# Forgetting attention and a GELU layer on one core: a new order of loads, casts, masks and fillers in the opening stage

## The chip, the cores and the metric

The kernel runs on one core of a Trainium2 chip. The core has five engines with a queue each: TensorE (PE in the profile; PEld are its weight loads), VectorE (DVE), ScalarE (ACT), GpSimd (POOL) and SyncE (SP). Each works through its own queue in order; semaphores between them make an instruction wait for another engine's result or for a DMA. The metric is the device time of one execution in microseconds; less is better.

## What is computed

For 8 batches of 8 heads, 576 tokens and head dimension 64, attention with a forget gate is computed; its output, as 4608 tokens of 512 features, goes through a two-layer network with a hidden width of 2048. Both matter here, since the network's first tokens are computed while the attention of later heads still runs.

```python
scores = scale * np.matmul(q, k.transpose(0, 1, 3, 2))
log_f = np.log(np.clip(f, 0.0001, 1.0))
cum = np.cumsum(log_f, axis=-1)
decay = cum[:, :, :, None] - cum[:, :, None, :]
scores = np.where(causal, -1000000000.0, scores + decay)
attn = softmax(scores)                       # over the keys
x = np.matmul(attn, v)                       # then (batch * seq, heads * dim)
...
h = x @ w_in
g = 0.5 * h * (1.0 + np.tanh(c * (h + 0.044715 * h * h * h)))
return (g @ w_out).astype(np.float32)
```

## The kernel before, in words

**Attention by quads.** A quad is four heads of one batch; quads 0 and 1 are batch 0, quads 2 and 3 batch 1, and so on to quad 15. The decay splits into a factor of the query, which cancels in the softmax, and a weight of the key, `exp(-cum)`. The kernel keeps these weights as `wT` (float32) and, rounded, as `w_bf` (bf16), and multiplies the values by them (`vw`). So a quad's result is a product of the exponentials (`pt`) with `vw`, divided by a product of `pt` with `w_bf`. For a quad TensorE computes scores into PSUM (`ps_s`, line 261), ScalarE turns them into `pt` (line 269), the blocks on the diagonal are masked either by GpSimd (`affine_select`, line 275) or by VectorE as a product with a triangle (line 304), and TensorE multiplies again (line 315 for quads 0 and 1, which are cut into a half 0 of 256 tokens and a half 1 of 320; line 329 for the others). VectorE makes the reciprocals of the denominators with two transpositions (`den`, line 348, and `rb`, line 352) and writes the result, times `rb`, to `xT` (line 360). Queries and keys come as `q_c` and `k_c` and are transposed by VectorE (line 197).

**The network by chunks** of 512 tokens. The first layer of chunk 0 is computed by halves and by four groups of hidden features (line 491, and line 514 for the piece that is copied to `snap` first), with GELU on ScalarE; its second layer is `mlp_out` (line 626): 4 row tiles of 16 products each, copied by VectorE and stored through SyncE. Later chunks use other functions that the change does not touch.

**An order written out by hand.** The scheduler is off. `setup()` issues the first loads and preparations, then `run(FRONT)` (line 781) goes through a table of words and issues each word's instructions to their engines' queues, so that the order of words is the order in each queue; words of different engines do not hold each other except by data. A word with `@` makes its first instruction wait also for the instruction kept under the name that follows. The words that the change and the prediction name:

- `B.n.c`: n filler products without use, c columns wide (line 239), on TensorE. Set-up issues 13 of its own.
- `Z`: zeros (line 675), copied by ScalarE from a zero tile into parts of `w_bf`, `vw` and `v_nat`. `CU`, `CW`, `SB`: the running sums of log f on TensorE and GpSimd and the exponentials that give `wT`. `W`: the cast of `wT` to `w_bf` on VectorE (line 724), of all quads, or with `.0` of quads 0 and 1, with `.1` of the others.
- `TQ.i`, `TK.i`: transposition of quad i's queries or keys. `LQ.i`, `LK.i`: their loads, issued by GpSimd.
- `LP.t`: load of tile t (128 tokens) of batch 0's values, issued by GpSimd; `LX`, `LV`: values of later batches, by GpSimd or SyncE. `WI.c`: one of 8 slices of `w_in` (two make a group of hidden features), `WO.c`: one of 4 quarters of `w_out`, both by GpSimd. Every load that GpSimd issues goes into one queue.
- `S.i.r`, `H.i.r.g`, `Q.i.r.g`: scores of quad i in round r with their exponentials, whole or by two heads.
- `M.i.r`: masks on GpSimd; `m.i.r`: masks on VectorE.
- `D.i`: denominators of quad i (product on TensorE, reciprocals on VectorE); `D.i.h` of half h. `V.i.x`, `v.i.x`, `V.i.x.h`: one of the two halves of the head dimension of the result, product on TensorE and the product with `rb` on VectorE.
- `vw.i`, `VW.i`: weighting of quad i's values on VectorE or GpSimd (line 214); with `.0` tiles 0 and 1, with `.1` tiles 2 to 4. `CL.i`: a copy within `vw` on VectorE.
- `h`, `j`, `J`, `E`: parts of chunk 0's first layer, its held pieces and their GELU. `F.c.n`, `f.c.n`: n products' worth of chunk c's second layer; `I`, `U`, `G`, `K`: of chunk 1.

PSUM tiles come from small pools: `psS` has two tiles of scores, `psO` one, `psM` two (`po_m`, `ps_q`, `pso`). A product into a new tile waits until the tile's former content has been read.

Of the kernel before, what the change touches and what calls it, by code (L numbers as in the profile page):

```python
# [16 lines left out]
def kernel(  # L17
# [192 lines left out]
    def make_vw(i, eng, part=None):  # L210
        h0 = 4 * (i % QPB)
        vb = v_nat[(i // QPB) % 2]
        t0, t1 = {None: (0, NT), 0: (0, QA // 128), 1: (QA // 128, NT)}[part]
        eng.tensor_mul(  # L214
            vw[i % 2][:, t0:t1], vb[:, t0:t1, h0:h0 + 4, :],
            wT[:, i, t0:t1, :].unsqueeze(3).to_broadcast([128, t1 - t0, 4, D]))
# [78 lines left out]
    def mask_by_product(i, r, keys=None):  # L295
        p = pt[i % 2]
        if i < 2:
            todo = [(0, col, n) for (key, col, n) in diagonals(r, keys)]
# [4 lines left out]
        for (m, col, n) in todo:
            nc.vector.tensor_mul(p[:, :, col:col + n], p[:, :, col:col + n],
                                 causal[m][:, 0:n].unsqueeze(1).to_broadcast([128, 4, n]))
# [339 lines left out]
    def setup():  # L645
# [16 lines left out]
        nc.vector.tensor_scalar(f_sb, f_sb, 1e-4, 1.0, op0=ALU.max, op1=ALU.min)
# [195 lines left out]
```

## Time and profile before

| what | value |
|---|---|
| median of 3 runs (lowest to highest) | 321.47 us (321.04 to 322.42) |
| the profiled execution | 321.33 us |
| its span, first to last instruction | 319.6 us |
| granted TensorE clock, mean | 0.999 |
| instructions | 12355 |

The profile is that of one execution. Its times are counted from the first instruction, and the span leaves out some 1.7 us around it. A line of a timeline has the start, the time it took, the engine, the source line, the operation, what it writes and reads, the shape, and how many equal instructions were merged; in brackets stands the idle time before it and what ended it. Products on TensorE overlap: a row of many has the time from the first start to the last end, and the next row can start a little before that end.

### The profile page before, as it was taken

The page shows a single profiled execution, that of the slowest core. Times are in us where ns is not written, and L with a number is a line of the kernel's source. Part 1 is how long each engine was busy: PE and PEld are TensorE (multiplying, and loading weights), DVE is VectorE, ACT ScalarE, POOL GpSimd, SP SyncE. Part 2 cuts the span into 40 slices and gives each one's busy share as a digit, 9 for nine tenths or more (in the row PEclk, how much of TensorE's full clock was granted, in tenths as well). Part 3 has the DMA queues.
Part 4 walks back from the last instruction along what each step waited for, and adds up shares of the span by engine and source line. Part 5 has one row for each costly group of instructions (what it writes and reads, how often), then busy time and mean ns, then how long its engine had stood idle before and what let it go on. Part 6 is the DMA issues. An engine that isn't in the chain of part 4 may idle for free.

```text
span 319.6 us, 12355 instructions
## 1 busy us (share of the span) xinstructions
PE 311.4 (97%) x5527; PEld 218.9 (68%) x5547; DVE 250.6 (78%) x398; ACT 208.4 (65%) x265; POOL 113.1 (35%) x160
## 2 busy tenths in 40 slices
PE   7899999999999999999999999999999999999995
PEld 3467744545776477766867677768766798788784
DVE  4866049977789899779987898689868969886882
ACT  6895676676766786759756865778567844722730
POOL 8997465720500219501770068104710240000000
PEclk9999999999999999999999999999999999999999
DMA  7999999898104830791159512971120112003013
GB/s 124 233 168 203 206 238 253 157 177 185 40 14 126 143 66 17 149 213 41 37 100 209 93 37 72 198 132 37 37 68 0 37 37 68 3 34 100 0 35 98
DMA packets 47574, 33.45 MB, mean 105 GB/s; under 512 B 29857, under 2 KB 42273, under 8 KB 47521
## 3 DMA queue, kind: packets, MB, share of 16 engines
q0 software_dynamic: 9712, 15.99, 28.9%
q1 hardware_dynamic: 37664, 16.60, 20.1%
q8 instruction: 43, 0.70, 0.9%
q10 hardware_dynamic: 144, 0.07, 0.1%
q14 instruction: 11, 0.08, 0.1%
HBM read 36.85 MB, written 9.44 MB: 145 GB/s over the span
## 4 chain that ended last, share of the span: by engine, by line
PE 93%; DVE 2%; DMA 2%; issue 1%; ACT 0%; POOL 0%; DVEq 0%; POOLq 0%
PE ps_w L565 30%; PE ps_h L374 16%; PE po L329 9%; PE ps_s L261 9%; PE ps_cd L433 8%; PE ps_ab L433 6%; PE ps_h L491 4%; PE pso L635 3%; PE ps_h L388 2%; DMA q_c<-in_q_dram 2%; PE po_m L315 2%; DVE qT L197 1%; PE ps_q L514 1%; PE idle_ps L239 1%; ACT pt L269 0%
## 5 line engine op out<-in xcount | busy, mean ns | idle before, releaser
L269 ACT ACTIVATE pt<-ps_s 128x1024 bf16<-128x1024 f32 (+2 forms) x98 | 92.3, 992 | 35.5 <-PE ps_s L261 31.9
L275 POOL TENSOR_SCALAR_AFFINE_SELECT pt<-pt 128x512 bf16<-128x512 bf16 (+2 forms) x67 | 40.3, 611 | 103.6 <-ACT pt L269 102.5
L374 PE MATMUL ps_h<-xT,w_in_sb 128*128 128x512 bf16 x228 | 54.5, 379 | 0.6
L565 PEld LDWEIGHTS <-gT 128*32 128x32 bf16 (+1 forms) x1247 | 50.6, 97 | 5.9 <-issue 1.7
L565 PE MATMUL ps_w<-w_out_sb,gT 128*32 128x256 bf16 (+1 forms) x1050 | 46.9, 273 | 0.0
L381 ACT ACTIVATE gT<-ps_h 128x1024 bf16<-128x1024 f32 x30 | 30.6, 1019 | 17.2 <-PE ps_h L374 16.7
L565 PEld LDWEIGHTS <-gsum 128*32 128x32 bf16 (+1 forms) x1256 | 39.3, 97 | 1.4
L374 PEld LDWEIGHTS <-w_in_sb 128*128 128x128 bf16 x240 | 23.4, 98 | 24.3 <-issue 0.4
L261 PE MATMUL ps_s<-qT,kT 32*128 32x448 bf16 (+5 forms) x880 | 35.4, 262 | 1.7 <-DVE qT L197 1.2
L214 POOL TENSOR_TENSOR vw<-v_nat,wT 128x1280 bf16<-128x1280 f32 (+1 forms) x13 | 29.8, 2291 | 3.8 <-DMA v_nat<-in_v_dram 3.4
L565 PE MATMUL ps_w<-usum,gsum 128*32 128x256 bf16 (+1 forms) x832 | 30.6, 273 | 0.0
L197 DVE STREAM_TRANSPOSE kT<-k_c 128x576 f32<-128x576 f32 x16 | 19.9, 1246 | 12.6 <-DMA k_c<-in_k_dram 12.6
L261 PEld LDWEIGHTS <-kT 32*128 32x128 bf16 x896 | 16.3, 92 | 18.5 <-issue 13.3
L442 ACT ACTIVATE gT<-snap 128x512 bf16<-128x512 f32 x45 | 26.1, 625 | 3.0 <-DVE snap L456 2.4
L590 DVE TENSOR_TENSOR o_st<-ps_w,snap 128x512 f32<-128x512 f32 x31 | 21.3, 686 | 8.3 <-PE ps_w L565 7.2
L433 PEld LDWEIGHTS <-w_in_sb 128*128 128x128 bf16 x240 | 23.4, 98 | 6.2 <-issue 1.5
L329 PE MATMUL po<-pt,vw 128*32 128x64 bf16 (+4 forms) x624 | 22.5, 278 | 0.3 <-DVE den L348 0.3
L360 DVE TENSOR_TENSOR xT<-po,rb 128x576 bf16<-128x576 f32 x26 | 19.5, 751 | 2.9 <-PE po L329 2.3
L329 PEld LDWEIGHTS <-vw 128*32 128x32 bf16 x672 | 14.5, 97 | 10.5 <-issue 4.4
L433 PEld LDWEIGHTS <-xT 128*128 128x128 bf16 x180 | 17.6, 98 | 5.2
L197 DVE STREAM_TRANSPOSE qT<-q_c 128x576 f32<-128x576 f32 x16 | 19.9, 1244 | 0.5 <-DMA q_c<-in_q_dram 0.5
L191 POOL DMA_DIRECT2D k_c<-in_k_dram x16 | 9.2, 577 | 25.0 <-DVE qT L197 21.0
(111 smaller groups left out, 482.8 us busy)
## 6 DMA issues: line engine op xcount, KB each, us to landing
out_dram<-o_st SPq DMA_DIRECT2D x35, 256.0 KB, 2.3
k_c<-in_k_dram POOLq DMA_DIRECT2D x16, 288.0 KB, 6.0
q_c<-in_q_dram POOLq DMA_DIRECT2D x16, 288.0 KB, 6.4
v_nat<-in_v_dram SPq DMA_DIRECT2D x16, 256.0 KB, 6.5
v_nat<-in_v_dram SPq DMA_DIRECT2D x20, 128.0 KB, 5.2
w_in_sb<-in_moe_w_in_dram POOLq DMA_DIRECT2D x8, 256.0 KB, 7.2
w_out_sb<-in_moe_w_out_dram POOLq DMA_DIRECT2D x4, 512.0 KB, 9.7
v_nat<-in_v_dram POOLq DMA_DIRECT2D x9, 128.0 KB, 5.9
```

What stands on the lines that cost most here:

```text
L197: nc.vector.transpose(out=dst.rearrange("p s c -> p (s c)").bitcast(FP32) .rearrange("p (t a) -> p a t", a=S // 32), in_=src.rearrange("p ...
L214: eng.tensor_mul(vw[i % 2][:, t0:t1], vb[:, t0:t1, h0:h0 + 4, :], wT[:, i, t0:t1, :].unsqueeze(3).to_broadcast([128, t1 - t0, 4, D]))
L261: nc.tensor.matmul(tiles[h // 2][:, h % 2, c0:c0 + nq], key_columns(i, key, h, c), qq[32 * h:32 * h + 32, q0:q0 + nq, c], start=(c == 0 an ...
L269: nc.scalar.activation(p[:, 2 * g:2 * g + 2, off:off + n], t[:, :, 0:n], AF.Exp, scale=scale)
L275: nc.gpsimd.affine_select(out=x, in_=x, compare_op=ALU.is_ge, fill=0.0, base=0, pattern=pattern, channel_multiplier=-1)
L329: nc.tensor.matmul(po[r0:r0 + w.shape[-1], 448 + q0:448 + q0 + nq], w, p[:, h, col:col + nq], start=(key in (0, "low")), stop=(key in ("lo ...
L374: nc.tensor.matmul(ph[:, j, :], w_in_sb[:, dt, 128 * ft:128 * ft + 128], xT[:, dt, CH * c:CH * (c + 1)], start=(dt == 0), stop=(dt == N_DT ...
L381: nc.scalar.activation(gT[:, 2 * pr:2 * pr + 2, :], ph, AF.Gelu_apprx_tanh)
L433: nc.tensor.matmul(ps[:, j], w[:, dt, 128 * j:128 * j + 128], x[:, dt], start=(first and j == 0 and dt == 0), stop=(dt == 1), skip_group_c ...
L442: nc.scalar.activation(gT[:, ft:ft + 2, HC * j:HC * (j + 1)], x, AF.Gelu_apprx_tanh)
L565: nc.tensor.matmul(ps[c0:c0 + width, n, cols[0]:cols[1]], x[:, j, 128 * n + c0:128 * n + c0 + width], w[:, j, cols[0]:cols[1]], start=(fir ...
L590: nc.vector.tensor_add(st, ps, kept[name])
```

## The change

Five things are done.

1. The zeros are written by five memsets of VectorE within `setup()`, ahead of the clamp of f, in place of ScalarE's five copies; the word `Z` is gone.
2. On GpSimd's queue `LP.4` is issued ahead of the masks `M.0.0`, `WI.3` ahead of the masks of quad 1, and `LP.3` behind these and in front of `WI.4`.
3. On VectorE, `W` casts quads 0 and 1 alone at first; the others' cast comes behind half 1 of batch 0. `vw.0.1` goes behind the two copies of `ps_q`. Quad 2's denominators go ahead of `TK.4` and `TQ.4`. Fillers are moved: one less ahead of `S.0.0`, two more behind `CW`, one less behind `D.1.0`.
4. `mlp_out` starts two row tiles at once: 12 products of each, then the last 4 of each; the other two as before. The words `F.0.n` between the scores of quad 2 are cut anew (6, 10, 9, 10 become 7, 9, 10, 9).
5. Quad 3's masks of round 0 are on GpSimd (`M.3.0`, two masks) in place of VectorE (`m.3.0`). `m.3.1` on VectorE comes sooner in the table, and `VW.3`, the weighting on GpSimd, waits for it by a semaphore; `CL.3` follows later.

```diff
     SETUP = """
-        Z.1.2 TK.0 LP.0 LP.1
+        TK.0 LP.0 LP.1
     """
     FRONT = """
-        TQ.0 B.3.384 TR TK.1 SB Z.0.3.4 CU B.3.384 S.0.0 CW H.0.2.0 H.0.2.1 B.6.384 TQ.1 W WI.0 WI.1 vw.0.0 LP.2@LQ.0 M.0.0 LP.4 LP.3 WI.2 H.1.0.1
-        H.1.0.0 vw.1.0 M.1.0.1 M.1.0.0 WI.3 WI.4 WI.5 D.0.0 B.2.384 H.1.1.1 V.0.0.0 H.0.1.1 V.0.1.0 H.0.1.0 D.1.0 B.1.384 V.1.0.0 M.0.1 WI.6 WI.7
-        H.1.1.0 M.1.1 V.1.1.0 Q.0.3.0 vw.0.1 h.0.0.0 h.0.0.0 M.0.3 LQ.2 LK.2 Q.1.3.1 h.0.0.1 h.0.0.1 S.1.2 M.1.3 VW.1.1 WO.0 D.0.1 j.0.1 j.0.1 j.0.1
-        j.0.1 E.0.0 j.0.1 V.0.1.1 V.0.0.1 D.1.1 J.0.2 WO.1 V.1.1.1 V.1.0.1 J.0.3 J.1.0 WO.2@WI.7 WO.3 J.1.1 TQ.2 LK.3 LQ.3 J.1.2 J.1.3 LX.1.0@WO.0
-        LQ.4 TK.2 X F.0.6 LK.4 TK.3 S.2.0 M.2.0 LK.5 F.0.10 S.2.2 M.2.2 LX.1.1@WO.2 F.0.9 S.2.1 TQ.3 F.0.10 LV.2.0@LK.5 m.2.1 vw.2 TQ.4 TK.4 S.3.0
-        f.0.1 CL.2 LQ.5 VW.3 D.2 f.0.6 S.3.1 F.0.6 V.2.0 m.3.0 S.3.2 TK.5 LK.6 M.3.2 f.0.7 V.2.1 CL.3 S.4.1 m.3.1 LQ.6 F.0.6 TQ.5 H.4.2.1 D.3
+        TQ.0 B.3.384 TR TK.1 SB CU B.2.384 S.0.0 CW B.2.384 H.0.2.0 H.0.2.1 B.6.384 TQ.1 W.0 WI.0 WI.1 vw.0.0 LP.2@LQ.0 LP.4 M.0.0 WI.2 WI.3 H.1.0.1
+        H.1.0.0 vw.1.0 D.0.0 M.1.0.1 M.1.0.0 LP.3 WI.4 WI.5 B.2.384 H.1.1.1 V.0.0.0 H.0.1.1 V.0.1.0 H.0.1.0 D.1.0 V.1.0.0 M.0.1 WI.6 WI.7 H.1.1.0
+        V.1.1.0 M.1.1 Q.0.3.0 h.0.0.0 h.0.0.0 M.0.3 LQ.2 LK.2 Q.1.3.1 h.0.0.1 h.0.0.1 vw.0.1 S.1.2 M.1.3 VW.1.1 WO.0 D.0.1 j.0.1 j.0.1 j.0.1 j.0.1
+        E.0.0 j.0.1 V.0.1.1 V.0.0.1 D.1.1 J.0.2 WO.1 V.1.1.1 V.1.0.1 J.0.3 W.1 J.1.0 WO.2@WI.7 WO.3 J.1.1 TQ.2 LK.3 LQ.3 J.1.2 J.1.3 LX.1.0@WO.0
+        LQ.4 TK.2 X F.0.7 LK.4 TK.3 S.2.0 M.2.0 LK.5 F.0.9 S.2.2 M.2.2 LX.1.1@WO.2 F.0.10 S.2.1 TQ.3 F.0.9 LV.2.0@LK.5 m.2.1 vw.2 S.3.0 f.0.1 CL.2
+        LQ.5 M.3.0 D.2 TK.4 f.0.6 S.3.1 F.0.6 m.3.1 VW.3@m.3.1 V.2.0 TQ.4 S.3.2 TK.5 LK.6 M.3.2 f.0.7 V.2.1 S.4.1 LQ.6 F.0.6 TQ.5 CL.3 H.4.2.1 D.3
...
     def mlp_out(c):
-        for n in range(CH // 128):
+        tiles, late = {}, 3 * N_FT // 4
+        for (n, f0, f1) in ((0, 0, late), (1, 0, late), (0, late, N_FT), (1, late, N_FT), (2, 0, N_FT), (3, 0, N_FT)):
             r0 = CH * c + 128 * n
-            st = ostage_pool.tile([128, D_MODEL], FP32, name="o_st", tag="o")
-            pso = psM.tile([128, D_MODEL], FP32, name="pso", tag="m")
-            for ft in range(N_FT):
+            if f0 == 0:
+                tiles[n] = psM.tile([128, D_MODEL], FP32, name="pso", tag="m")
+            pso = tiles[n]
+            for ft in range(f0, f1):
...
                 if ft == N_FT - 1:
+                    st = ostage_pool.tile([128, D_MODEL], FP32, name="o_st", tag="o")
                     nc.vector.tensor_copy(st, pso)
...
-    def zeros(which):
-        todo = [(w_bf[0:64, :, LOW, :], idle[0:64, 0:BH].rearrange("p (i h) -> p i h", h=4))]
...
-        for n in which:
-            nc.scalar.copy(*todo[n])
+    def zeros():
+        nc.vector.memset(w_bf[0:64, :, LOW, :], 0.0)
+        for t_ in vw:
+            nc.vector.memset(t_[0:64, LOW, :, :], 0.0)
+        for t_ in v_nat:
+            nc.vector.memset(t_[64:128, HIGH, :, :], 0.0)
```

`make_vw` and `mask_by_product` now return their instructions, so that `VW.3@m.3.1` has something to tie together.

More of the change, by code (lines that the diff above doesn't have):

```diff
@@ L302, in mask_by_product @@
                     and rounds[r][0] <= col < rounds[r][0] + 512 and key != 0]
[L303 to L305 removed]
+        return [nc.vector.tensor_mul(p[:, :, col:col + n], p[:, :, col:col + n],
+                                     causal[m][:, 0:n].unsqueeze(1).to_broadcast([128, 4, n])) for (m, col, n) in todo]
     def product(i, groups, spare, part=None):
@@ L661, in setup @@
             nc.vector.memset(t_[:, 64 + S:], 0.0)
+        zeros()
         nc.vector.tensor_scalar(f_sb, f_sb, 1e-4, 1.0, op0=ALU.max, op1=ALU.min)
```

5 lines of the change are left out of this document (1 added, 4 removed).

## The prediction

> **What bounds the kernel now.** I read the engines' busy times and the chain first, then TensorE's instructions in order of time, then those of the engines that end its waits.
>
> ```profile
> PE 311.4 (97%) x5527; PEld 218.9 (68%) x5547; DVE 250.6 (78%) x398; ACT 208.4 (65%) x265; POOL 113.1 (35%) x160
> ...
> PE 93%; DVE 2%; DMA 2%; issue 1%; ACT 0%; POOL 0%; DVEq 0%; POOLq 0%
> ```
>
> TensorE is busy for 97% of the span and holds 93% of the chain that ended last. The change takes no product away, so it can only close gaps in TensorE's queue or open some. Every edit lies ahead of the first product of chunk 1 (about 64 us), so I look for gaps there.
>
> ```profile
> 1.26 3.92 PE L239 MATMUL idle_ps<-usum 128*128 128x384 bf16 x13 [1.26 <-DVE usum L654]
> ...
> 8.71 0.52 PE L261 MATMUL ps_s<-qT,kT 32*128 32x256 bf16 x16 [1.22 <-DVE qT L197]
> 9.17 0.70 PE L703 MATMUL cum_ps<-gsum 128*128 128x256 f32 x2
> 10.13 0.46 PE L261 MATMUL ps_s<-qT,kT 32*128 32x320 bf16 x4 [0.27 <-ACT pt L269]
> ...
> 11.22 1.15 PE L239 MATMUL idle_ps<-usum 128*128 128x384 bf16 x6
> ...
> 16.44 0.34 PE L239 MATMUL idle_ps<-usum 128*128 128x384 bf16 x1
> ...
> 18.30 1.04 PE L514 MATMUL ps_q<-xT,w_in_sb 128*128 128x256 bf16 x8
> ...
> 19.88 1.05 PE L514 MATMUL ps_q<-xT,w_in_sb 128*128 128x256 bf16 x8
> ...
> 21.30 0.96 PE L315 MATMUL po_m<-pt,w_bf 128*32 128x320 bf16 x20
> ...
> 25.36 0.70 PE L315 MATMUL po_m<-pt,w_bf 128*32 128x320 bf16 x20
> ...
> 48.69 0.85 PE L329 MATMUL po<-pt,w_bf 128*32 128x512 bf16 x24
> ...
> 53.08 0.87 PE L329 MATMUL po<-pt,vw 128*32 128x512 bf16 x24 [0.28 <-DVE den L348]
> ...
> 56.76 0.64 PE L261 MATMUL ps_s<-qT,kT 32*128 32x64 bf16 x16
> ...
> 59.28 0.87 PE L329 MATMUL po<-pt,w_bf 128*32 128x512 bf16 x24
> ```
>
> Columns: start, duration, instruction, count, and in brackets the idle time before it with what ended it. Two gaps stand where the change works. The 20 products of D.0.1 at 21.30 take 0.96 us and the same 20 of D.1.1 at 25.36 take 0.70 us, so 0.26 us of D.0.1 is waiting inside the group. V.2.0 at 53.08 waits 0.28 us for VectorE's denominators.
>
> **Term 1, the last mask ahead of D.0.1.** GpSimd and VectorE around it:
>
> ```profile
> 15.63 2.14 POOL L180 DMA_DIRECT2D w_in_sb<-in_moe_w_in_dram  x3
> 17.79 0.64 POOL L275 TENSOR_SCALAR_AFFINE_SELECT pt<-pt 128x512 bf16<-128x512 bf16 x1
> ...
> 19.81 1.24 POOL L275 TENSOR_SCALAR_AFFINE_SELECT pt<-pt 128x512 bf16<-128x512 bf16 x1
> ...
> 19.81 2.21 POOL L275 TENSOR_SCALAR_AFFINE_SELECT pt<-pt 128x512 bf16<-128x512 bf16 x3
> ```
> ```profile
> 17.83 0.76 DVE L360 TENSOR_TENSOR xT<-po_m,rb 128x256 bf16<-128x256 f32 x2
> 19.60 0.96 DVE L214 TENSOR_TENSOR vw<-v_nat,wT 128x768 bf16<-128x768 f32 x1 [1.01 <-DMA v_nat<-in_v_dram]
> 20.47 1.28 DVE L519 COPY snap<-ps_q 128x512 f32<-128x512 f32 x2
> 22.32 0.52 DVE L348 STREAM_TRANSPOSE den<-po_m 128x320 f32<-128x320 f32 x1 [0.56 <-PE po_m L315]
> ...
> 23.12 0.51 DVE L352 STREAM_TRANSPOSE rb<-rec 128x320 f32<-128x320 f32 x1
> 24.81 1.01 DVE L360 TENSOR_TENSOR xT<-po_m,rb 128x320 bf16<-128x320 f32 x2 [1.18 <-PE po_m L315]
> ```
>
> M.1.1 at 19.81 takes 1.24 us where the equal mask at 17.79 takes 0.64. The last row is the same mask merged with the two of M.0.3, which follow without a pause: they end at 19.81 + 2.21 = 22.02, just where D.0.1 ends. M.1.1 ran while VectorE's vw.0.1 ran (19.60 to 20.56). The change puts vw.0.1 behind the two snapshot copies, the second of which cannot end before about 21.7 (its ps_q ends at 19.88 + 1.05 = 20.93; then half of 1.28 and a start). So M.1.1 no longer meets it. GpSimd's own queue gets later by one step: LP.3 (0.90, quoted below) goes between M.1.0 and WI.4, while WI.3 (2.14 / 3 = 0.71) goes ahead, so M.0.1 and all behind it start 0.2 later. Then M.1.1 runs from 20.0 to 20.6 and M.0.3 (2.21 - 1.24 = 0.97) to 21.6, against 22.02. D.0.1's last four products are due some 0.1 ahead of its end at 21.30 + 0.70. Gain: 0.26, all of it. Bounds: 0 if the mask is slow again, 0.26 at best.
>
> The row, 1.24 against 0.64, is what I price by. [...]
>
> **Cover that vw.0.1 loses.** It waits for LP.3, whose transfer now starts 2.9 us later:
>
> ```profile
> 12.73 0.90 POOL L168 DMA_DIRECT2D v_nat<-in_v_dram  x1
> ...
> w_in_sb<-in_moe_w_in_dram POOLq DMA_DIRECT2D x1, 256.0 KB, 5.8
> ...
> DMA to landing us min/median/max: 5.9/7.2/7.9
> ```
>
> The second row is WI.3 alone, issued at 15.63 and landed 5.8 later, at 21.4; the third is over all values' loads of the first 30 us. LP.3 takes WI.3's place in the queue with the same bytes ahead of it, so I take 21.5 (bounds 21.4, and 15.63 + 7.9 = 23.5). Behind vw.0.1 on VectorE stand D.0.1's denominators, whose reciprocals V.0.1.1's result waits for, whose PSUM tile D.1.1 waits for: from the landing L, 0.96 (vw.0.1), 23.12 + 0.51 - 22.32 = 1.31, half of 1.01, and 0.05 to D.1.1: L + 2.82. D.1.1 is due at 25.36 - 0.26 = 25.10, so L up to 22.28 costs nothing. At 21.7 (the copies, not L) the margin is 0.6. On GpSimd, VW.1.1 waits for L too, but its result is first used near 28. WI.3 and the later slices are not late; nothing else moves in the queue.
>
> **Term 2, denominators of quad 2 first.**
>
> ```profile
> 49.63 1.25 DVE L197 STREAM_TRANSPOSE qT<-q_c 128x576 f32<-128x576 f32 x1
> 51.99 0.22 DVE L219 COPY vw<-vw 64x256 bf16<-64x256 bf16 x1
> 52.25 0.78 DVE L348 STREAM_TRANSPOSE den<-po 128x576 f32<-128x576 f32 x1
> ...
> 55.31 1.13 DVE L304 TENSOR_TENSOR pt<-pt,causal 128x512 bf16<-128x512 bf16 x1
> ...
> 53.83 2.33 POOL L214 TENSOR_TENSOR vw<-v_nat,wT 128x1280 bf16<-128x1280 f32 x1 [3.37 <-DMA v_nat<-in_v_dram]
> ...
> 56.71 1.24 POOL L275 TENSOR_SCALAR_AFFINE_SELECT pt<-pt 128x512 bf16<-128x512 bf16 x2
> ```
>
> With TQ.4 and TK.4 behind it, the transposition of the denominators moves up by 51.99 - 49.63 = 2.36, to 49.9, and ends near 50.7 (D.2's products end at 48.69 + 0.85 and don't hold it). TensorE reaches V.2.0 at 53.08 - 0.28 = 52.80. Gain 0.28, with 2 us to spare. The pairs put one product more (0.2) ahead of S.2.1 and one less behind it, so D.2 keeps its place. What is late next: TQ.4. Its new order is TK.4, the third store copy, m.3.1, V.2.0's result, TQ.4; by the durations of before it ends near 55.8, and S.4.1 needs it at 56.76 - 0.54 = 56.2: covered by 0.4. VW.3 now waits for m.3.1, which ends near 53.8; it started at 53.83 before, held by its DMA. Behind it on GpSimd stand LK.6 and M.3.2, done near 57.95 as before; D.3 wants them at 59.28 - 0.54 = 58.7. M.3.0's two masks fill part of GpSimd's 3.37 us of idling. The 1.13 us of m.3.0 leave VectorE, where TensorE does not wait for them: 0.
>
> **Terms that I set to nothing.** The zeros: five memsets ahead of the clamp of f.
>
> ```profile
> 1.36 0.33 DVE L656 MEMSET gsum<- 128x320 f32 x1
> ...
> 3.65 0.45 DVE L662 TENSOR_SCALAR gsum<-gsum 64x576 f32<-64x576 f32 x1 [1.38 <-DMA gsum<-in_f_dram]
> ...
> 4.13 0.68 ACT L663 ACTIVATE gsum<-gsum 64x576 f32<-64x576 f32 x1 [2.04 <-DVE gsum L662]
> ...
> 6.89 1.11 POOL L691 TENSOR_TENSOR gsum<-gsum 128x64 f32<-128x64 f32 x3
> ...
> 42.19 1.26 DVE L197 STREAM_TRANSPOSE kT<-k_c 128x576 f32<-128x576 f32 x1 [10.32 <-DMA k_c<-in_k_dram]
> ```
>
> At 0.33 per 320 elements they take some 1.4 us of the 1.38 us in which VectorE waited for f, so the logarithm ends at 4.8 to 4.9, still under the 13 filler products (to 5.18). At twice the price the transposes behind the fillers would start at 6.2, 1.0 late, and GpSimd's running sums would end at 8.00 + 1.0 = 9.0, still ahead of the product of 9.17 that takes them. The five copies leave ScalarE ahead of exponentials that wait for TensorE anyway. 0 at both ends.
>
> The fillers behind the set-up's 13 are 15 before and after: one less ahead of S.0.0 (idle there anyway), two more at 9.9 where 0.27 us was idle, and one less at 16.44. That last one seems a gain of up to 0.34, but ps_q at 18.30 needs the PSUM tile and xT of 17.83 + 0.38, which depend on D.1.0, ahead of the filler. So 0 (end -0.34). The casts: 14 of 16 quads' weights move behind half 0's results, in front of TQ.2 and TK.2; behind these VectorE idles for 10.32 us, and S.2.0, which wants them after the whole first layer of chunk 0, lies inside that stretch. The second layer by pairs issues the same products with the same copies and stores; the last quarter of w_out is asked for later, not earlier, and S.2.0 and S.2.2 keep 16 products ahead of or between them, as before. 0.
>
> **The sum.** The profiled execution took 321.33 us (span 319.6, so 1.7 around it), 0.14 under the median of 321.47. 321.33 - 0.26 - 0.28 = 320.8.
>
> **Rivals.**
> *One gain does not arrive* (the change doing only half of what it says): M.1.1 is slow again, or GpSimd's extra 0.2 eats it, or V.2.0 waits elsewhere. For it: the margin of the last mask is only 0.3. Against it: the overlaps are plain. 321.33 - 0.27 = 321.1.
>
> *The late values win*, the other side: L decides. From L = 22.28 D.1.1 slips; at 22.82 both gains are gone. At L = 23.5 D.1.1 starts at 26.32, 0.96 late, and with V.2.0's 0.28 the run is at 322.0. For it: the median, 7.2, gives L = 22.8. Against it: the load in that very place took 5.8.
>
> *The clock falls.* The idle stretch ahead of S.0.0 grows from 1.22 to about 1.4 us. At the start 13 fillers took 3.92 us, 0.30 each; at 11.22 six took 1.15, 0.19 each. A slow stretch of 3.9 us from 12.3 on would cost up to 3.9 x (1 - 0.19 / 0.30) = 1.4 us: 322.2. Against it: 1.22 us of idling changed nothing.
>
> **How the numbers follow.** Forecast 0.62, half a gain 0.20, late values 0.14, clock 0.04. The likeliest alone spans 320.4 to 321.2 (0.3 to either side of 320.8 for the costs above, and a little more). For 8 in 10 I take 320.1 to 322.2: beyond it lie the worst of the late values and runs that differ as the three of before do (321.04 to 322.42). About 0.5%, 1.6 us, is what a measurement of this kernel can tell from no change. No gap in the first 64 us is large enough for a gain of that size: faster 0.06. Slower by it takes L beyond 24.5, the clock together with a lost gain, or something that these rows don't show: 0.11. The rest, 0.83, is no change.
>
> **What would show it.** Right: D.0.1's 20 products in some 0.70 us, M.1.1 in 0.62, V.2.0 without idle time before it, and vw.0.1 starting near 21.7 behind the copies. Wrong: vw.0.1 with idle time before it that ends by the DMA of the values after 22.3, a D.1.1 later than 25.4, an idle stretch ahead of S.4.1 or D.3, or a granted clock under 1 after 8.7 us. If both gains are there and the time is not down by half a microsecond, something behind 64 us takes it back.

## The result and the profile after

| | before | after |
|---|---|---|
| median of 20 executions each, same chip | 321.45 us (320.74 to 323.43) | 320.75 us (320.29 to 325.23) |
| ratio, 95% interval | | 0.9972 (0.9958 to 0.9985) |
| executions over 321.7 us | 8 of 20 | 3 of 20 |
| median of the others | 321.09 us | 320.62 us |
| profiled execution, its span, granted clock | 321.33, 319.6, 0.999 | 322.00, 320.3, 0.995 |

The median fell by 0.7 us, 0.2%: no change by the bound of 0.5%, and 0.05 from the forecast of 320.8. (A disturbed execution, 325.23, is left out of the ratio.) The interval leaves out 1, so the gain is small but more than chance. The two rows on executions over 321.7 us say that it is two things: a typical execution became 0.47 shorter, and there are fewer long ones. The profiled execution of the kernel after is one of the long ones, so its absolute starts must not be compared with those of before. TensorE in order of time and a table by windows show why (start, duration, count; for the windows: length, busy time of TensorE and its weight loads, VectorE, ScalarE, GpSimd, then the granted clock, DMA share, GB/s):

```profile
11.15 2.10 PE L239 MATMUL idle_ps<-usum 128*128 128x384 bf16 x6
13.18 0.85 PE L261 MATMUL ps_s<-qT,kT 32*128 32x256 bf16 x16
```
```profile
8.00:10.80 2.80, 2.08 (x28) 1.01 (x27) 1.91 (x5) 1.76 (x4) 2.80 (x5) 0.99 1.08 249
10.80:14.20 3.40, 3.40 (x34) 1.29 (x30) 2.64 (x5) 1.63 (x5) 2.87 (x5) 0.50 1.14 197
14.20:18.00 3.80, 3.71 (x72) 1.98 (x66) 2.57 (x7) 3.79 (x5) 2.37 (x4) 1.00 1.18 211
```

Six filler products take 2.10 us where they took 1.15 before, and the granted clock is 0.50 for 3.4 us. From S.0.0 to the first ps_q this execution takes 19.35 - 8.48 = 10.87; a repetition at full clock (e1, below) takes 18.03 - 8.21 = 9.82. So one such fall costs 1.05 us here (0.9 to 1.4 against the other profiles at full clock, which take 9.45 to 9.97). Behind it, differences between starts are sound. TensorE, VectorE and GpSimd of the kernel after around D.0.1:

```profile
19.35 1.03 PE L513 MATMUL ps_q<-xT,w_in_sb 128*128 128x256 bf16 x8 [0.34 <-DVE xT L359]
...
22.21 0.80 PE L314 MATMUL po_m<-pt,w_bf 128*32 128x320 bf16 x20
...
26.09 0.70 PE L314 MATMUL po_m<-pt,w_bf 128*32 128x320 bf16 x20
...
53.49 0.87 PE L328 MATMUL po<-pt,vw 128*32 128x512 bf16 x24
...
60.48 1.46 PE L261 MATMUL ps_s<-qT,kT 32*128 32x64 bf16 x24
61.87 0.86 PE L328 MATMUL po<-pt,vw 128*32 128x512 bf16 x24
```
```profile
21.86 0.69 DVE L518 COPY snap<-ps_q 128x512 f32<-128x512 f32 x1 [0.74 <-PE ps_q L513]
22.46 1.52 DVE L214 TENSOR_TENSOR vw<-v_nat,wT 128x768 bf16<-128x768 f32 x1
23.91 0.50 DVE L347 STREAM_TRANSPOSE den<-po_m 128x320 f32<-128x320 f32 x1
```
```profile
16.82 0.90 POOL L168 DMA_DIRECT2D v_nat<-in_v_dram  x1
...
21.15 1.60 POOL L275 TENSOR_SCALAR_AFFINE_SELECT pt<-pt 128x512 bf16<-128x512 bf16 x3
```

D.0.1 takes 0.80 (0.96 before) and V.2.0 at 53.49 has no idle time before it (0.28 before): both gains are there. M.1.1 and M.0.3 together take 1.60 (2.21). But vw.0.1 itself now takes 1.52 where it took 0.96, and the group of scores ahead of V.3.1 takes 1.46 us in place of 1.14. Nothing waits for the first; the second costs. TensorE waits there for ScalarE, whose row, with the chain of waits of the same stretch (start, time, what), is:

```profile
57.82 1.94 ACT L269 ACTIVATE pt<-ps_s 128x1024 bf16<-128x1024 f32 x2 [0.87 <-PE ps_s L261]
60.17 2.06 ACT L269 ACTIVATE pt<-ps_s 128x1024 bf16<-128x1024 f32 x2 [0.41 <-PE ps_s L261]
```
```profile
59.19 0.58 PE ps_s L261 x8
...
59.81 0.36 issue
60.17 1.03 ACT pt L269
```

ScalarE was free at 57.82 + 1.94 = 59.76 and the scores of H.4.2.1 ended at 59.77; its exponential started at 60.17. The chain calls the 0.36 us between them "issue": time in which the engine waited for nothing that the profile shows. Before, the same exponential started 0.09 after its scores.

Five starts on TensorE are the same work in every kernel: the first ps_q, D.0.1, D.1.1, V.2.0 and V.3.1. The times between them, from the rows of each kernel's profiled execution, are what the rest of this text goes by:

| kernel | ps_q to D.0.1 | to D.1.1 | to V.2.0 | to V.3.1 | sum |
|---|---|---|---|---|---|
| before | 3.00 | 4.06 | 27.72 | 8.07 | 42.85 |
| after | 2.86 | 3.88 | 27.40 | 8.38 | 42.52 |
| e1 after again | 2.86 | 3.86 | 27.40 | 8.38 | 42.50 |
| e2 vw.0.1 moved alone | 2.99 | 3.85 | 27.90 | 8.08 | 42.82 |
| e3 denominators first alone | 2.99 | 3.79 | 27.38 | 8.06 | 42.22 |
| e4 after, vw.0.1 back | 4.49 | 3.79 | 27.39 | 8.37 | 44.04 |
| e5 after, zeros back | 2.86 | 3.87 | 27.40 | 8.06 | 42.19 |
| e6 after, quad 3 back | 2.87 | 3.86 | 27.40 | 8.79 | 42.92 |
| e7 after, LP.3 later | 2.86 | 6.81 | 28.70 | 8.37 | 46.74 |
| e8 after, two fillers fewer | 2.86 | 3.88 | 27.39 | 8.74 | 42.87 |
| e9 e5 with before's loads | 2.86 | 3.79 | 27.81 | 8.06 | 42.52 |
| e10 before with three edits | 2.99 | 3.79 | 27.38 | 8.06 | 42.22 |
| e11 before again | 3.00 | 3.79 | 28.76 | 8.40 | 43.95 |
| e12 before again | 3.00 | 3.79 | 27.72 | 8.06 | 42.57 |

Behind V.3.1 nothing takes the gain back: from there to the end of the span these kernels take 258.4 to 258.7 us, e6 alone, at a granted clock of 0.998, 259.1.

### The profile page after: what moved, and what is told of

It reads as the page before. It is cut to its first block, busy times and chain, and to the rows that moved or that the text cites. A ratio compares the mean times of both kernels' runs of the same rounds, so it can differ in the third digit from the quotient of the medians.

```text
span 320.3 us, 12376 instructions
## 1 busy us (share of the span) xinstructions
PE 313.1 (98%) x5547; PEld 218.5 (68%) x5547; DVE 252.1 (79%) x403; ACT 206.5 (64%) x260; POOL 113.9 (36%) x162
## 4 chain that ended last, share of the span: by engine, by line
PE 94%; DMA 2%; DVE 1%; ACT 1%; issue 1%; POOL 0%; DVEq 0%; ACTq 0%; POOLq 0%
PE ps_w L564 30%; PE ps_h L373 16%; PE ps_s L261 9%; PE po L328 9%; PE ps_cd L432 8%; PE ps_ab L432 6%; PE pso L636 5%; PE ps_h L490 4%; PE ps_h L387 2%; DMA q_c<-in_q_dram 2%; PE po_m L314 1%; ACT pt L269 1%; PE idle_ps L239 1%; PE ps_q L513 1%; PE ps_o L328 0%
```

## The experiments

The kernels ran in four sessions, each on one chip beside the kernel before: e1 to e4 (median of before 321.79), e5 to e8 (321.40), e9 and e10 (321.48), e11 and e12 (one execution of before, 322.53).

**e1: the kernel after once more.**

> The changed kernel again, for a profile without the clock's fall that its first profile shows (the six fillers ahead of quad 1's scores took 2.10 us there against 1.15, at a granted clock of 0.50). My theory: both gains are in this profile. D.0.1's 20 products take 0.70 us (0.96 before), V.2.0 has no idle time before it, and the time is 0.5 to 0.6 us under the kernel before, a ratio near 0.998. Rival: the gain is one of fewer clock falls only; then the 20 products or V.2.0 still wait, and a run with a steady clock is within 0.2 us of the kernel before.

Median 320.88 us, ratio 0.9977 (0.9959 to 0.9995); span 318.9, clock 1.0. D.0.1 took 0.78 us and not the expected 0.70. The clock did not fall, and everything else is as in the first profile: sum 42.50, the exponential of H.4.2.1 0.41 late again. So the late exponential belongs to the kernel, the fall of the clock to an execution.

**e2 and e3: one gain alone.** Each is the kernel before with one piece of the order changed.

```diff
- Q.0.3.0 vw.0.1 h.0.0.0 h.0.0.0 M.0.3 LQ.2 LK.2 Q.1.3.1 h.0.0.1 h.0.0.1 S.1.2
+ Q.0.3.0 h.0.0.0 h.0.0.0 M.0.3 LQ.2 LK.2 Q.1.3.1 h.0.0.1 h.0.0.1 vw.0.1 S.1.2
```

> The kernel before with one word moved: the weighting vw.0.1 goes behind the two copies of ps_q; loads, masks and denominators stay as before. My theory: M.1.1 takes 0.62 to 0.64 us in place of 1.24, D.0.1 some 0.70 in place of 0.96, the time falls by 0.2 to 0.3 us. If the slow mask had another cause than vw.0.1 running beside it, it stays at 1.2 and the time does not change. If the loads' new order is what counts, nothing changes either.

```diff
- vw.2 TQ.4 TK.4 S.3.0 f.0.1 CL.2 LQ.5 VW.3 D.2 f.0.6 S.3.1 F.0.6 V.2.0 m.3.0
+ vw.2 S.3.0 f.0.1 CL.2 LQ.5 VW.3 D.2 TK.4 f.0.6 S.3.1 F.0.6 V.2.0 TQ.4 m.3.0
```

> The kernel before with quad 2's denominators ahead of TK.4 and TQ.4 alone; quad 3's first mask stays on VectorE (m.3.0) and VW.3 waits for no semaphore. My theory: V.2.0's idle time of 0.28 us goes. But m.3.0 now stands behind TQ.4 and meets VW.3 on GpSimd, and m.3.1 still comes late, so VectorE reaches m.3.1 near 59.1 and D.3, due near 59.0, waits 0.1 to 0.3 us for it: net between -0.28 and 0. Rival: the masks are in time without the move of m.3.0 and the semaphore; then -0.28 in full.

e2: 321.13 us, ratio 0.9987 (0.9968 to 1.0006). e3: 322.44, 1.0008 (0.9987 to 1.0029). By the times neither is told from no change. By the table, e3 shows the whole of term 2 (27.38 against 27.72), and e2 keeps the idle 0.28 of V.2.0, as it must. (Its 27.90 is longer than before's because V.1.1.1's 40 products took 1.40 us and not 1.22, without a wait that the profile names.) For term 1 the pair taught something else: D.0.1 took 0.70 us in e3 too, where vw.0.1 is where it always was. Its values had landed at 17.98 in place of 19.48, vw.0.1 was over before M.1.1 began, and there was nothing to gain. Of the four profiled executions with vw.0.1 in the old place and before's loads (before, e3, e11, e12) only the first shows D.0.1 at 0.96. Term 1 is a gain in some executions, not in all. And 7 of e3's 12 executions took over 321.7 us, which neither term explains.

**e4: vw.0.1 back, the late load kept.** An edit of the kernel after.

```diff
- Q.0.3.0 h.0.0.0 h.0.0.0 M.0.3 LQ.2 LK.2 Q.1.3.1 h.0.0.1 h.0.0.1 vw.0.1 S.1.2
+ Q.0.3.0 vw.0.1 h.0.0.0 h.0.0.0 M.0.3 LQ.2 LK.2 Q.1.3.1 h.0.0.1 h.0.0.1 S.1.2
```

> The changed kernel with vw.0.1 back in its old place, ahead of the copies of ps_q, the loads in their new order. My theory: VectorE stands still for the late slice of the values (landing near 21.3), weights it until 22.3, and only then makes the copies; the PSUM tile of the first copy comes free near 23.0, so D.0.1 starts near 23 in place of 21.3: slower than the changed kernel by 1.2 to 1.8 us, slower than before by about 1. If the slice lands early (under 19.5) nothing is lost but term 1: +0.26.

323.86 us, ratio 1.0065 (1.0038 to 1.0092). VectorE, then TensorE:

```profile
20.61 0.96 DVE L214 TENSOR_TENSOR vw<-v_nat,wT 128x768 bf16<-128x768 f32 x1 [2.59 <-DMA v_nat<-in_v_dram]
21.50 1.28 DVE L518 COPY snap<-ps_q 128x512 f32<-128x512 f32 x2
```
```profile
22.23 0.70 PE L314 MATMUL po_m<-pt,w_bf 128*32 128x320 bf16 x20 [1.55 <-DVE snap L518]
```

vw.0.1 waits 2.59 us for its DMA and holds both copies behind it; D.0.1 waits 1.55 for them. So loading the values later needs using them later; using them later does not need the late load, as e2 shows. The median is not the wait's doing alone: 6 of the 11 executions had a granted clock of 0.995 or less, and the profiled one, at 0.999, took 322.03.

**e5: the zeros back on ScalarE.** My first theory of the late exponential was the new order of quad 3's masks. The rival: the change took five copies out of ScalarE's queue, so every later instruction stands five places further forward. e5 and e6 tell them apart.

```diff
-        zeros()
- TK.0 LP.0 LP.1
+ Z.1.2 TK.0 LP.0 LP.1
- TQ.0 B.3.384 TR TK.1 SB CU
+ TQ.0 B.3.384 TR TK.1 SB Z.0.3.4 CU
```

> The kernel after, with the five zero fills copied by ScalarE again as before (two in the set-up, three between the running sums and S.0.0) and not by VectorE's memsets. It tests two things. First, the term set to nothing: the memsets should be worth 0 either way, so TensorE reaches S.0.0 within 0.4 us of the kernel after. Second, the pause that is new in the kernel after: H.4.2.1's exponential starts 0.40 us after ScalarE is free and its scores are there (0.09 in the kernel before), and V.3.1's group of scores takes 1.46 us in place of 1.14, with 0.24 us of TensorE waiting for an exponential. Theory A (position in ScalarE's queue: five instructions fewer ahead of it put a pause of its own, of about 0.3 us, on this exponential): with the five copies back the exponential starts within 0.1 us, the scores at about 59 us take 1.14 us, and the time is 0.24 below the kernel after, 320.5 to 320.7. Theory B (order of quad 3's masks on GpSimd): the exponential is again 0.40 us late and the scores take 1.46 us; time as the kernel after.

320.70 us (320.29 to 321.15, none of 12 over 321.7), ratio 0.9971 (0.9954 to 0.9989). ScalarE, then TensorE:

```profile
56.79 3.05 ACT L269 ACTIVATE pt<-ps_s 128x1024 bf16<-128x1024 f32 x3 [0.88 <-PE ps_s L261]
```
```profile
59.44 1.14 PE L261 MATMUL ps_s<-qT,kT 32*128 32x64 bf16 x24
60.51 0.87 PE L328 MATMUL po<-pt,vw 128*32 128x512 bf16 x24
```

Three exponentials run in one row without the 0.41, the scores take 1.14 and not 1.46, and V.2.0 to V.3.1 takes 8.06. The five copies, which I had set to nothing, are worth 0.32 us where they are. They also cost nothing at the start: S.0.0 at 8.35, against 8.21 in e1 and 8.48 in the kernel after's first profile.

**e6: quad 3's masks as before.**

```diff
- LQ.5 M.3.0 D.2 TK.4 f.0.6 S.3.1 F.0.6 m.3.1 VW.3@m.3.1 V.2.0 TQ.4 S.3.2 TK.5 LK.6 M.3.2 f.0.7 V.2.1 S.4.1 LQ.6 F.0.6 TQ.5 CL.3
+ LQ.5 VW.3 D.2 TK.4 f.0.6 S.3.1 F.0.6 V.2.0 TQ.4 m.3.0 S.3.2 TK.5 LK.6 M.3.2 f.0.7 V.2.1 CL.3 S.4.1 m.3.1 LQ.6 F.0.6 TQ.5
```

> The kernel after, with quad 3's masks as before: m.3.0 by VectorE's products behind TQ.4, no wait of VW.3 for m.3.1, the copy CL.3 ahead of S.4.1; the denominators of quad 2 still come first. Theory A (position in ScalarE's queue, which has the same number of instructions as in the kernel after): H.4.2.1's exponential is still 0.40 us late and the scores at about 59 us take 1.46 us. Theory B (quad 3's order on GpSimd and VectorE): the exponential starts within 0.1 us and the scores take 1.14 us. In both, V.2.0 starts without idle time; by A the time is that of the kernel after (0 within 0.2 us), by B 0.24 less.

321.77 us, ratio 1.0003 (0.9984 to 1.0022). The exponential is again 0.41 late: theory B is out, and the pause goes with the five copies, as A has it. One thing in the records lies near it. Between 55 and 64 us one block of 8 KB is fetched on a DMA queue for instructions: at 60.7 to 62.0 in after, e1, e4, e6 and e8 (63.7 in e7), and at 55.2 to 57.4 in the kernels with the copies. The queue's rows in windows of e1 (60.0 to 61.6) and of e5 (55.0 to 57.6):

```profile
q14 instruction: 1, 0.01, 1.5%
```
```profile
q14 instruction: 1, 0.01, 0.8%
```

But the fetch comes too late to be what this exponential waits for: in e1 it starts at 60.66, and the exponential started at 58.83. Nor is a fixed place in the queue shown. The late exponential is ScalarE's 64th recorded instruction; with the copies the 64th starts without a pause, and the next one stands behind 0.88 us of waiting for TensorE (e5's row), which could hide one. So what is shown is that the pause comes and goes with the five copies (and the memsets in their place); what it is stays open.

But e6 was 1.07 us slower than e5 beside it, which neither theory foresaw; the late exponential is 0.32 of that. VectorE, GpSimd and TensorE:

```profile
54.93 1.80 DVE L303 TENSOR_TENSOR pt<-pt,causal 128x512 bf16<-128x512 bf16 x1
```
```profile
54.12 2.33 POOL L214 TENSOR_TENSOR vw<-v_nat,wT 128x1280 bf16<-128x1280 f32 x1 [3.60 <-DMA v_nat<-in_v_dram]
```
```profile
59.28 0.61 PE L328 MATMUL po<-pt,w_bf 128*1 128x448 bf16 x16 [0.31 <-DVE pt L303]
...
61.03 0.87 PE L328 MATMUL po<-pt,vw 128*32 128x512 bf16 x24 [0.27 <-DVE den L347]
```

With the denominators first, m.3.0 stands behind TQ.4 and meets VW.3 on GpSimd: it takes 1.80 us (1.13 before; 0.79 in e3, where VW.3 was nearly over), everything behind it on VectorE is late, and D.3 and V.3.1 wait 0.31 and 0.27. So the masks' part of the change, M.3.0 on GpSimd and VW.3 behind m.3.1, is what makes term 2 safe. It isn't worth nothing, as I had it. e3 has the order of e6, but its long executions lie some 1.9 us above its short ones, more than this meeting costs in e6 (0.41), so it does not explain them by itself.

**e7: the values later still.**

```diff
- M.1.0.0 LP.3 WI.4 WI.5 B.2.384
+ M.1.0.0 WI.4 WI.5 LP.3 B.2.384
```

> The kernel after, with the load of the late values (LP.3) issued two places later, behind WI.4 and WI.5, 1.4 us later. By the formula of the prediction D.1.1 starts at L + 2.82 once the values land (L) behind 22.28, and D.0.1 does not move at all. The values landed at 21.14 with 4.3 us of flight in the kernel after, so L should be 22.3 to 24.5 here: VectorE's product of the values (vw.0.1) waits for its DMA, and the time grows by 0 to 2 us, with D.1.1 at L + 2.82. The rival (GpSimd and not the values sets D.1.1, since VW.1.1 waits for the same landing and the issues of w_out and of the keys stand behind it): D.1.1 starts without regard to L and the delay shows later, at the products of quad 1's second half or at the first layer's slices.

324.83 us (6 executions), ratio 1.0114 (1.0074 to 1.0153). VectorE, GpSimd and TensorE:

```profile
23.30 2.23 DVE L214 TENSOR_TENSOR vw<-v_nat,wT 128x768 bf16<-128x768 f32 x1 [2.36 <-DMA v_nat<-in_v_dram]
```
```profile
23.25 1.47 POOL L214 TENSOR_TENSOR vw<-v_nat,wT 128x768 bf16<-128x768 f32 x1
```
```profile
25.59 1.13 PE L314 MATMUL po_m<-pt,vw 128*32 128x320 bf16 x32 [1.95 <-DVE vw L214]
27.40 0.99 PE L314 MATMUL po_m<-pt,w_bf 128*32 128x320 bf16 x12 [0.69 <-DVE xT L359]
```

The values landed at 23.17 and D.1.1 started at 27.40: L + 4.23, not L + 2.82. Its direction and its first wait are the formula's; one term was wrong. VW.1.1 on GpSimd waits for the same landing, starts 0.05 before vw.0.1, and vw.0.1 takes 2.23 in place of 0.96: 1.27 of the 1.41 missing. I had also not seen that V.0.1.1 itself reads vw and waits 1.95; that wait lies within D.1.1's delay and adds nothing to it, since D.1.1 then still waits 0.69 for VectorE. The granted clock fell as well, to 0.53 in the 3.5 us behind these waits, and 5 of the 6 executions had 0.995 or less, so the 3.9 us over e1's median are not all the values' doing.

**e8: two fillers fewer ahead of S.0.0.**

```diff
- CU B.2.384 S.0.0 CW B.2.384
+ CU S.0.0 CW B.2.384
```

> The kernel after without the two filler products between the running sums and S.0.0, so that TensorE idles 0.6 us more there (1.2 to 1.9 us in place of 0.7 to 1.2). Nothing waits for fillers, so by the work alone the time is the same. If it is this idling that lets the clock fall, many executions show a mean granted clock of 0.995, 3.4 us at half clock between 10 and 15 us, and a time of 321.6 to 322.2 (the kernel after's own profiled execution: 322.0, with six filler products of 2.10 us in place of 1.15); the median then rises by 0.5 to 1.3 us. If the fall has nothing to do with it, the share of executions at 0.995 stays at some 2 in 20 and the median within 0.2 us.

321.00 us, ratio 1.0001 (0.9969 to 1.0033); 2 of 12 executions at a granted clock of 0.995, both near 324.9. The profiled one idled 1.19 us ahead of S.0.0 at full clock throughout. The expected rise of 0.5 to 1.3 did not come: this idling alone does not bring the fall. (The two near 324.9 lie 3.9 us above the median, more than the 1.05 us, at most 1.4, that 3.4 us at half clock cost in the kernel after's profile; neither was profiled, so what else they waited for is not known.) (The profile's sum is 0.37 above e1's for another reason: VW.3's values landed at 55.28, 1.4 later than in e1, and D.3 waited for the masks behind it on GpSimd.)

**e9: e5 with the loads in before's order.**

```diff
- LP.2@LQ.0 LP.4 M.0.0 WI.2 WI.3 H.1.0.1 H.1.0.0 vw.1.0 D.0.0 M.1.0.1 M.1.0.0 LP.3 WI.4 WI.5
+ LP.2@LQ.0 M.0.0 LP.4 LP.3 WI.2 H.1.0.1 H.1.0.0 vw.1.0 D.0.0 M.1.0.1 M.1.0.0 WI.3 WI.4 WI.5
```

> The kernel of e5 (the kernel after with the zeros copied by ScalarE) with the load of the late values and the slices of the first layer in before's order (LP.3 ahead of WI.2, WI.3 behind quad 1's first masks). GpSimd then reaches M.1.1 0.2 us earlier, so by my theory D.0.1's 20 products take 0.70 us in place of 0.77, the values land 2 to 3 us earlier (near 19.5), and vw.0.1 still runs at 21.2 behind the copies: 320.6, 0.1 under e5, and no execution above 322 at full clock. Rival (the slice WI.3 has to come first, since products wait for it): a wait of TensorE for a DMA of w_in appears between 18 and 33 us, and the time is 0.3 or more above e5.

320.93 us, ratio 0.9982 (0.9962 to 1.0003). D.0.1 took 0.70, as expected: the 0.08 that the kernel after loses in this group comes with the loads' new order, by GpSimd's 0.2. TensorE lost 0.41 us at V.1.1.1 (1.63 against 1.22; 27.81 in the table), as in e2 without a wait that the profile names, so the time is no better than e5's. No wait for a slice of w_in appeared either.

**e10: before with three edits alone**: vw.0.1 as in e2, TQ.4 and TK.4 away from ahead of S.3.0 as in e3, and quad 3's masks as in the kernel after.

```diff
- LQ.5 VW.3 D.2 f.0.6 S.3.1 F.0.6 V.2.0 m.3.0 S.3.2 TK.5 LK.6 M.3.2 f.0.7 V.2.1 CL.3 S.4.1 m.3.1 LQ.6 F.0.6 TQ.5
+ LQ.5 M.3.0 D.2 TK.4 f.0.6 S.3.1 F.0.6 m.3.1 VW.3@m.3.1 V.2.0 TQ.4 S.3.2 TK.5 LK.6 M.3.2 f.0.7 V.2.1 S.4.1 LQ.6 F.0.6 TQ.5 CL.3
```

> The kernel before with three edits alone: vw.0.1 behind the four first-layer groups, the denominators of quad 2 ahead of TQ.4 and TK.4, and quad 3's masks as in the kernel after (M.3.0 on GpSimd, m.3.1 on VectorE ahead of VW.3's wait, CL.3 behind TQ.5). Zeros, fillers, casts, loads and the second layer of chunk 0 stay as before. My theory, that all else in the change is worth 0, expects e5's or e9's time: 320.6 to 320.8, V.2.0 without idle time, D.0.1 in 0.70, H.4.2.1's exponential 0.09 us after its scores. Rival (the pairs of the second layer, the fillers or the casts carry part of the gain): 0.2 or more above both, with the gap to be seen ahead of S.0.0, at 10 to 13 us, or between 42 and 53 us.

320.90 us (320.65 to 321.17), ratio 0.9966 (0.9949 to 0.9982): as good as the whole change, and not told apart from e5. So the new zeros, casts, loads and pairs are not needed for its time, and none of its 12 executions was long. In the table it wins 0.08 on e5 at D.0.1 and loses 0.13 in the first column. That column splits all fourteen kernels by their fillers: 2.86 or 2.87 where the filler of 16.44 is gone, 2.99 or 3.00 where it stands, and e4, which waits for the late copies, apart. The casts and the pairs moved in the same kernels, so the column alone does not tell them from the filler; ScalarE's rows in e10 and in e1 speak for the filler:

```profile
17.50 1.02 ACT L269 ACTIVATE pt<-ps_s 128x1024 bf16<-128x1024 f32 x1 [0.28 <-PE ps_s L261]
18.43 0.81 ACT L269 ACTIVATE pt<-ps_so 128x768 bf16<-128x768 f32 x1
```
```profile
16.07 2.06 ACT L269 ACTIVATE pt<-ps_s 128x1024 bf16<-128x1024 f32 x2
18.03 0.81 ACT L269 ACTIVATE pt<-ps_so 128x768 bf16<-128x768 f32 x1
```

With the filler, ScalarE idles 0.28 for H.1.1.0's scores, and the exponential that frees the tile ps_so ends at 18.43 + 0.81 = 19.24; Q.1.3.1's products in that tile start at 19.28, 0.16 behind those in the other tile. Without it both start at 19.00.

**e11 and e12: what the long executions wait for.** By then 47 of 106 executions of the kernel before had taken over 321.7 us. Two single executions of it, unchanged.

> The kernel before once more, for what its longer executions wait for: 47 of 106 of its executions so far took over 321.7 us, against 8 of 68 of the five kernels with vw.0.1 behind the first-layer groups and the denominators first (after, its repetition, e5, e9, e10). Theory: the values (LP.3) land late, vw.0.1 holds the two snapshot copies behind it on VectorE, and D.0.1 waits for the copies. Then an execution over 321.7 shows vw.0.1 starting after 20.2 (relative to the products of ps_q at 18.3) and idle time ahead of D.0.1 that ends by a snapshot copy, and one under it shows neither. Rival: the load of quad 3's values (VW.3) lands late and D.3 waits for GpSimd's masks near 59; then D.0.1 is as usual and the idle time stands ahead of or in D.3.

> The kernel before a second time, with the same expectation as e11: over 321.7 us with vw.0.1 after 20.2 and a wait of D.0.1 for a snapshot copy, or by the rival with a wait of D.3 for GpSimd's masks.

Both were long, 322.28 and 322.41, and neither by the theory or the rival. TensorE in e11 (granted clock 0.999):

```profile
39.62 1.24 PE L635 MATMUL pso<-w_out_sb,gT 128*128 128x512 bf16 x5
41.98 1.02 PE L635 MATMUL pso<-w_out_sb,gT 128*128 128x512 bf16 x4 [1.11 <-DMA w_out_sb<-in_moe_w_out_dram]
```

The second layer of chunk 0 waits 1.11 us for the last quarter of w_out. The loads of w_out in before, e11 and e1 (count, shortest, median and longest issue in ns, first and last start; then the time from DMA to landing):

```profile
L184 POOL DMA_DIRECT2D w_out_sb<-in_moe_w_out_dram x4: 740/751/811, 25.5 to 29.0; - x4
...
DMA to landing us min/median/max: 7.7/9.7/11.8
```
```profile
L184 POOL DMA_DIRECT2D w_out_sb<-in_moe_w_out_dram x4: 742/754/813, 25.0 to 29.3; - x4
...
DMA to landing us min/median/max: 9.3/10.9/12.7
```
```profile
L184 POOL DMA_DIRECT2D w_out_sb<-in_moe_w_out_dram x4: 740/752/811, 24.9 to 28.2; - x4
...
DMA to landing us min/median/max: 8.4/10.2/12.4
```

The last quarter lands at 29.0 + 11.8 = 40.8 in before, 29.3 + 12.7 = 42.0 in e11, 28.2 + 12.4 = 40.6 in e1. The kernel before asks for it behind 12 products, at 41.06 in its profile: 0.3 us of cover. The kernel after, which runs two tiles' first three quarters and then their last ones, asks behind 24 products, at 44.03 in e1: 3.4 us. e11 lost another 0.33 at V.3.1 (8.40 in the table), by the meeting that e6 showed, here in the old order; VectorE:

```profile
55.97 1.87 DVE L304 TENSOR_TENSOR pt<-pt,causal 128x512 bf16<-128x512 bf16 x1
```

m.3.0 took 1.87 us, VW.3 ran on GpSimd from 55.23 to 57.56. In e12 the clock fell:

```profile
8.73 0.52 PE L261 MATMUL ps_s<-qT,kT 32*128 32x256 bf16 x16 [1.52 <-DVE qT L197]
...
11.36 2.10 PE L239 MATMUL idle_ps<-usum 128*128 128x384 bf16 x6
```
```profile
10.90:14.30 3.40, 3.40 (x30) 1.33 (x33) 3.12 (x5) 1.81 (x5) 3.40 (x5) 0.52 1.14 192
```

The same six products at 2.10 and the same 3.4 us at half clock as in the kernel after's own profile. So there are two kinds of long execution, at full clock and at a lowered one. By e11's rows the change should remove both waits of the first kind: the pairs give w_out its cover, and m.3.1's place ahead of VW.3 with M.3.0 on GpSimd ends the meeting. For the pairs this is argued and not shown. No kernel has them alone or the change without them, and e10, without them, had no long execution although its last quarter landed just as late in its profile (28.5 + 12.0 = 40.5, 0.1 to 0.2 us before it was asked for). By the counts both kinds became rarer: 5 of 56 executions of after, e1, e5 and e9 are long at full clock (22 of 86 of before, beside e1 to e10) and 3 of 56 at a clock of 0.995 or less (17 of 86).

## Why the prediction was right, and where it was not

The forecast was 321.33 - 0.26 - 0.28 = 320.8; a typical execution fell by 0.47 and the median by 0.70. The time and the two waits named were right, but the sum was right partly by terms that cancel, and the median came so near it only because there were also fewer long executions, which the prediction did not have. That part is luck. From ps_q to V.3.1, before against e1, 42.85 - 42.50 = 0.35:

| step of the prediction | it said | measured |
|---|---|---|
| term 1, D.0.1 | -0.26 | -0.20 (4.06 to 3.86) against before's profile; 0.07 the other way (3.79 to 3.86) against e11 and e12, where D.0.1 did not wait |
| term 2, V.2.0 | -0.28 | -0.32 (27.72 to 27.40) |
| the filler at 16.44 | 0, end -0.34 | -0.14 (3.00 to 2.86) |
| zero copies off ScalarE | 0 at both ends | +0.31 (8.07 to 8.38) |
| second layer by pairs | 0 | 0 in the execution profiled; up to -1.1 in one like e11, worked out from its wait and not tested alone |
| masks of quad 3 | 0 | up to -0.3 in one like e11, and 0.4 kept off that e6 lost (8.79 against 8.38) |

The table's 0.35 stands beside a typical execution's 0.47 in the first comparison and 0.29 in e1's session (321.11 to 320.82, both medians of the executions up to 321.7).

*Term 1.* The row 1.24 against 0.64 was priced as the meeting of M.1.1 with vw.0.1, and M.1.1 and M.0.3 indeed went from 2.21 to 1.60. But the meeting was not removed, it changed sides: vw.0.1 now starts at 21.15 in e1 while the last mask runs (19.82 to 21.41) and takes 1.52. The step that failed is "M.1.1 no longer meets it": right for M.1.1, silent about M.0.3. It cost nothing, for D.1.1 had the room. What did cost is the other half of the same step, GpSimd's extra 0.2, which was to fit under D.0.1's last products: D.0.1 took 0.78 in e1 and 0.70 in e9, without that 0.2, so 0.08 of the 0.26 never came. In three rows the one that started second took, to 0.15 us, what was left of the first and its own undisturbed time: the mask behind vw.0.1 (before) 1.24 against 0.75 + 0.64, vw.0.1 behind VW.1.1 (e7) 2.23 against 1.42 + 0.96, and m.3.0 behind VW.3 (e6) 1.80 against 1.52 + 0.42, the time of m.3.1 there. The fourth, vw.0.1 with 1.52 (e1), agrees in direction; what was left of the mask, 0.26, and its own 0.96 make 1.22, and the other 0.3 is not explained. What holds the second one is not shown.

*The cover of vw.0.1.* L was 20.4 in e1 and 21.1 in the kernel after's profile against 21.5 predicted, under the 22.28 from which it costs. The form L + 2.82 was right in direction and 1.4 short at L = 23.17 (e7), because its term for vw.0.1 was the undisturbed 0.96. The rival of the late values did not happen; e7 shows that two places in GpSimd's queue would have brought it on, and dearer than I had it.

*Term 2* came as told, V.2.0's idle time gone with 2 us to spare (e1, e3, e5, e10 all 27.4). What the prediction got wrong is that m.3.0's leaving VectorE was set to nothing, "where TensorE does not wait for them": in e6 and e11 TensorE does, since m.3.0 takes 1.80 and 1.87 there and not 1.13.

*The filler.* "ps_q at 18.30 needs the PSUM tile and xT" was right, and its wait for xT is there (0.34 in the kernel after's profile). But TensorE isn't the only user of the freed time: ScalarE's exponentials moved forward with H.1.1.0, by 0.27 us counted from the first ps_q (18.43 - 18.16 against 18.03 - 18.03), and freed ps_so earlier. (The other quads' casts stand behind half 1's results, at 28.9 in e1, and not behind half 0's as the prediction has it; its 0 for them holds.)

*The zeros.* The step "the five copies leave ScalarE ahead of exponentials that wait for TensorE anyway" looked at what the copies delay. It did not look at what moves when a queue gets shorter. It is the largest error, 0.31 us, and it hid in the sum because the filler and the long executions made up for it.

*The pairs.* "The last quarter of w_out is asked for later, not earlier" was the right fact, and I drew 0 from it because the one execution I had showed no wait there. A cover of 0.3 us behind a transfer of 12 us was the row to look at. In e2's profile it is already gone: the last quarter landed at 28.6 + 11.9 = 40.5, and the row of ten products there takes 2.46 us in place of 2.33. How many of the long executions it explains is open, and the counts do not speak for the pairs: of the kernels that keep before's second layer, e2 had 3 of 12 over 321.7, e3 7 of 12, but e10 none of 12; of those with the pairs and no other harm (after, e1, e5, e9) 8 of 56. Of before's executions beside e1 to e10 17 of 86 were long at a clock of 0.995 or less and 22 of 86 at 0.998 or more.

*The rival of the clock* had 0.04 and 322.2. It came true in the very execution that was profiled, 322.00, and at about its price (1.05, bound 1.4). Its condition was wrong: the idling ahead of S.0.0 did not grow to 1.4 us but was 1.07, and behind 1.19 us of it in e8 and 1.22 in before no fall followed (e8's profile has a clock of 1.0, before's record full clock from 4.83 to 318.86). What I had missed stands in the traces' records of the granted clock. In after one of 6.83 us at full clock, one of 3.41 at half and one of 307.20 at full follow each other, and in before one at full clock lasts 314.03: 2, 1, 90 and 92 times 3.413. By the granted shares in their windows the falls of e12 and e7 lasted 3.4 us too, from 11.04 and from 26.82. In the 3.41 us just ahead of the fall TensorE was busy for 2.10 (after), 1.79 (e12) and 1.38 (e7). In before it was busy for as little as 1.71 of the 3.40 us from 7.40, and no fall followed. Counted in lengths of 3.41 from the start of that record at 4.83, one ends at 8.25, in the middle of the idling, and the two have 2.66 and 2.44. That it matters where the idling lies against such lengths, and not only how long it is, is my estimate from these rows; no run tests it. A bare share does not settle it, for in e4 3.00 us with 1.77 busy (from 21.0) were followed by 12 us at 1.00. In the two kernels whose profiles show TensorE waiting for 1.55 us (e4) and 1.95 us (e7), 6 of 11 and 5 of 6 executions had a clock of 0.995 or less.

No kernel tried is clearly better than the change. e5, the change with the zeros left on ScalarE, is 0.31 us shorter from ps_q to V.3.1; 320.70 against 320.88 for e1 in another session does not tell them apart by time.

## What to carry to other kernels

A margin read from one execution is one draw: where a transfer of 12 us is covered by 0.3 us, ask how far its landing varies before setting the edit that adds cover to nothing, and look at the spread of the times before the median. Five copies taken out of ScalarE's queue moved everything behind them five places forward, and a pause of 0.3 us came to stand at a critical exponential. Before moving an operation away from another engine's, follow it to where it lands: there it meets the next one.

## What I had not expected of the hardware

A pause of some 0.3 us on ScalarE comes and goes with five copies that stand 50 us earlier in its queue: six profiled kernels without them (after, e1, e4, e6, e7, e8) start the same exponential 0.40 to 0.41 us after ScalarE is free, and the eight with them 0.09. Its cause is not known. On VectorE vw.0.1 stretched from 0.96 us (before) to 1.52 (after, e1) or 2.23 (e7) when GpSimd was ahead of it, and GpSimd's mask from 0.64 to 1.24 (before) when VectorE was: in these rows the one that starts second pays. The granted clock fell to 0.50 for 3.41 us in the profile of the kernel after, which cost 0.9 to 1.4 us there and left a mean of 0.995 (half of 3.4 in 320), and 18 of 86 executions of before had that or less.
